# A written issue order for five engines in an attention, MoE and MLP kernel on one Trainium2 core

## The chip, the core and the metric

The kernel runs on one core of one Trainium2 chip. The core has five engines that run side by side, each working through its own instructions in the order in which they were issued: TensorE (PE: matrix products; the loads of its weights are shown apart as PEld), VectorE (DVE), ScalarE (ACT), GpSimd (POOL), and SyncE (SP), which here does nothing but issue transfers. Sixteen DMA engines carry the transfers between HBM and the core's memory. An instruction that waits for another engine's result holds up all that is queued behind it on its own engine.

The metric is the device time of one execution in microseconds, lower is better.

## What is computed

Causal attention with a forgetting bias, then a gated MLP behind an RMS norm, then a second MLP. The sizes are 4 batches, 8 heads, 576 positions, head width 64; a model width of 512; inner widths of 1536 and 2048; so 2304 tokens.

```python
def _attn_ref(q, k, v, s):
    scores = scale * np.matmul(q, k.transpose(0, 1, 3, 2))
    cum = np.cumsum(np.maximum(s, 0.0), axis=-1)
    bias = -(cum[:, :, :, None] - cum[:, :, None, :])
    scores = np.where(causal, -1000000000.0, scores + np.minimum(bias, 0.0))
    attn = np.exp(scores - np.max(scores, axis=-1, keepdims=True))
    attn = attn / (np.sum(attn, axis=-1, keepdims=True) + 1e-09)
    return np.matmul(attn, v)

def _moe_ref(x, w_gate, w_val, w_out, rms_g):
    xn = x / np.sqrt(np.mean(x * x, axis=-1, keepdims=True) + 1e-06) * rms_g
    g = xn @ w_gate
    return (g * (1.0 / (1.0 + np.exp(-g)))) * (xn @ w_val) @ w_out

def _moe2_ref(x, w_in, w_out):
    h = x @ w_in
    return (h - np.tanh(h)) @ w_out
```

## The kernel before

All products are made in 16-bit floats. A 32-bit operand is split into a high part and a small remainder, and a product becomes three matmuls into one sum: high by high, high by remainder, remainder by high (`mm3`, L693 to L695). The weights arrive as 64-bit floats. VectorE turns each piece of 128 x 512 into 32-bit floats with three integer instructions (`decode`, L559 to L561), ScalarE squares it for the scale, and after a scale for the group is known, ScalarE writes the high part (L575) and VectorE the remainder (L576).

The program has three layers of work that overlap.

- **Attention** goes over 20 query tiles T (five in a batch, four of 128 rows and one of 64). For a tile, `prep_q` scales q and splits it (L364 to L368); `emit_smax` makes the scores once to find the row maxima (matmuls L399 to L416 into tiles `sm`, reduced on VectorE at L403, L411 or L417); `emit_rt` splits the maxima (L427, L428), turns them (L431) and lets SP copy them into rows of the q operand (`qc<-rt`, L434); `emit_st` makes the scores again, transposed and less the maxima (L452, L453), ScalarE takes the exponential (L460, L467), GpSimd masks and makes the remainder (L462, L474); `emit_pv` multiplies with v (L494 to L498); `emit_x` and `emit_norm` divide, normalise and split the rows (L513 to L546), and two transposing transfers (L547, L548) bring them into `xth` and `xtl` (tiles of a block of 384 tokens). K of the next batch is scaled and split by `conv_head` (L289 to L291, where VectorE's L291 waits for a copy that SP makes at L290).
- **The gated MLP** runs in six blocks of 384 tokens (`up1_g`, `up1_v`, `down1`). For each of 12 column groups f, a gate tile takes 12 matmuls of 384 columns into one PSUM bank; ScalarE takes its tanh (L711) and VectorE multiplies (L712), which frees the bank. A value tile takes 12 matmuls into another bank, freed by VectorE at L722. There are two such banks while attention runs (`ps_mm`), so the gate tile of f+1 uses the bank of gate tile f. `down1` makes four tiles of 36 matmuls (freed by ScalarE, L733). Blocks 0 to 4 run beside attention of the following tiles, block 5 after it.
- **The second MLP** follows in six blocks: the first two plainly (`up2`, `down2`), then two pairs with a scheme that trades products for additions (`pair_up`).

Weight tasks (`wt`, `wot`, `w2t`) are pushed in between. Weights of the gated MLP are needed by block 0, so their decoding runs in the first quarter of the program.

The order is set by a scheduler that lists the ready instructions by the order in which the code wrote them and by its own estimate of times (`schedule_with_timeline_sim=True`). Two things bind it further. `hold()` puts a transfer behind an earlier one on SP: each load of q, k and v behind the fourth last SP instruction written before it, the weight loads of `decode` behind the copy of the cumulative sums (`gate[0]`). And the second half of the first 16 weight tasks stands behind the last split of maxima:

```python
        with tc.issue_after(last_r[0]) if left[0] < 8 else ExitStack():
            run_tasks(wt, n)
```

Of the kernel before, what the change touches and what calls it, by code (L numbers as in the profile page):

```python
# [30 lines left out]
RSQRT_MAGIC = 1597463007.0 + 2.0 ** 30 - 2.0 ** 22  # L31
LN_P = 2.772588722239781
PAIR_16384 = float.fromhex("0x1.00e8p105")


def width(t):
    return 64 if t == 4 else 128
# [3 lines left out]
def tile_forget_attention_moe_moe2(ctx, tc, qa, qb, kt, va, vb, va0, vb0, s, wg, wv, wo, rg, win, wo2, out):  # L41
    nc = tc.nc
# [27 lines left out]
    V, A, G, P, SY = nc.vector, nc.scalar, nc.gpsimd, nc.tensor, nc.sync  # L70
# [24 lines left out]
    cpd = dram.tile([32, 3, S], FP16, name="cpd")  # L95
# [4 lines left out]
    def sm_tile(dtype=FP32):  # L100

        p, tag = (ps_mm, "mm") if early[0] else (ps_sm, "sm")
        return p.tile([128, 512], dtype, name=tag, tag=tag)

    wide = [None]
# [19 lines left out]
    def small(p, shape, dtype=FP32, tag=None):  # L125
        cnt[0] += 1
        return p.tile(shape, dtype, name=tag or f"sc{cnt[0]}", tag=tag or f"sc{cnt[0]}")
# [13 lines left out]
    def kc_consts(i):  # L141
        (V if i < 2 else G).memset(KC[i][0:64, 0:KW].bitcast(FP32), PAIR_16384)
        (V if i < 2 else G).memset(KC[i][:, KW:KPAD], 0.0)
        (V if i < 2 else G).memset(K2[i][:, KW:KPAD], 0.0)
# [30 lines left out]
    isig_c = const.tile([128, 1], I32, name="isig_c")  # L175

    cum = []
    gate = []

    def hold(kind=0):  # L180

        m = 4 if kind == 0 else 0 if wide[0] is None else 0
        if m == 0 or not gate:
            return tc.issue_after(gate[0]) if gate else ExitStack()
        k = m
        for ins in reversed(nc.cur_bb.bb.instructions):
            if ins.engine == SY.engine:
                k -= 1
                if k == 0:
                    return tc.issue_after(ins)  # L190
        return ExitStack()

    def emit_cum(st, CP):
        SY.dma_start(out=st[:, 0, :], in_=s)
# [23 lines left out]
    vstate = {}  # L218

    def load_qn(b, hh):  # L220
        with hold():
            return _load_qn(b, hh)

    def _load_qn(b, hh):
        t = stage_p.tile([128, 1152], FP32, name="stv", tag="stv", bufs=2)
        SY.dma_start(out=t[:, 0:1024], in_=qa[b, hh].rearrange("t (u d) h c -> (t u) (d h c)", u=32))
        SY.dma_start(out=t[:, 1024:1152], in_=qb[b, hh].rearrange("(u d) h c -> u (d h c)", u=2).rearrange("u (w c) -> (u w) c", w=64))
        return t

    def load_k(b):  # L230
        with hold():
            return _load_k(b)

    def _load_k(b):
        t = stage_p.tile([128, KW], FP32, name="stk", tag="stk", bufs=1)
        SY.dma_start(out=t, in_=kt[b].rearrange("r d h c -> (r d) (h c)"))
        return t

    def load_v(b, hh):
        with hold():  # L240
            return _load_v(b, hh)

    def _load_v(b, hh):
        t = stage_p.tile([128, 20, D], FP32, name="stv", tag="stv", bufs=2)
        SY.dma_start(out=t[:, 0:16, :], in_=va[b, hh].rearrange("p c h d -> p (c h) d"))
        SY.dma_start(out=t[0:64, 16:20, :], in_=vb[b, hh])
        return t
# [74 lines left out]
    qstage = {}  # L322

    def load_q(T):
        with hold():
            return _load_q(T)

    def _load_q(T):
        b, t = ORDER[T]
        w = width(t)  # L330
        if T in (1, 2):
            st = (KC, K2)[T - 1][2][:, 1024:2048].bitcast(FP32).rearrange("p (h c) -> p h c", h=NH)
        else:
            st = qst_p.tile([128, NH, 128], FP32, name="qst", tag="qst")
        for hh in range(2):
            src = qb[b, hh] if t == 4 else qa[b, hh, t]
            SY.dma_start(out=st[64 - 64 * hh:128 - 64 * hh, :, 0:w], in_=src)
        qstage[T] = st
# [6 lines left out]
    def qc_of(T):  # L345
        return spare(KC[2], 0) if T == 2 else QC[T % 2]
# [24 lines left out]


    rstate = {}
    last_r = [None]

    def smax_items(T):
        b, t = ORDER[T]
# [41 lines left out]
    def emit_rt(T):  # L419
        b, t = ORDER[T]  # L420
        rs = rstate.pop(T)
        n = H
        if t == 4:
            n = H // 2
            V.tensor_tensor(out=rs[0][:, 0:n], in0=rs[0][:, 0:n], in1=rs[1][:, 0:n], op=ALU.max)
        r2 = small(sm_p, [128, 2 * H], FP16, "r2")
        V.tensor_scalar(out=r2[:, 0:n], in0=rs[0][:, 0:n], scalar1=-1.0 / 16384.0, scalar2=None, op0=ALU.mult)  # L427
        V.scalar_tensor_tensor(out=r2[:, n:2 * n], in0=rs[0][:, 0:n], scalar=-1.0 / 16384.0, in1=r2[:, 0:n], op0=ALU.mult, op1=ALU.subtract)  # L428
        last_r[0] = nc.cur_bb.bb.instructions[-1]
        ps = sm_tile(FP16)  # L430
        P.transpose(ps[0:2 * n, 0:128], r2[:, 0:2 * n], ident)  # L431
        rt = small(sm_p, [2 * H, 128], FP16, "rt")
        A.activation(out=rt[0:2 * n], in_=ps[0:2 * n, 0:128], func=ACTF.Copy)
        SY.dma_start(out=qc_of(T)[0:2, :, 0:width(t)], in_=rt[0:2 * n, :])  # L434
# [116 lines left out]
    def decode(dst, src, raw):  # L551

        if src.dtype != I32:
            SY.dma_start(out=dst, in_=src)
            return
        with hold(1):
            SY.dma_start(out=raw, in_=src)
        d, hi, lo = dst.bitcast(I32), raw[:, :, 1], raw[:, :, 0]
        V.tensor_scalar(out=d, in0=hi, scalar1=3, scalar2=0x3FFFFFFF, op0=ALU.logical_shift_left, op1=ALU.bitwise_and)  # L559
        V.scalar_tensor_tensor(out=d, in0=hi, scalar=-0x40000000, in1=d, op0=ALU.bitwise_and, op1=ALU.bitwise_or)  # L560
        V.scalar_tensor_tensor(out=d, in0=lo, scalar=29, in1=d, op0=ALU.logical_shift_right, op1=ALU.bitwise_or)  # L561
# [186 lines left out]
    def run_tasks(lst, n):  # L748
        while n > 0 and lst:
            lst.pop(0)()  # L750
            n -= 1
# [123 lines left out]
    emit_consts()  # L875

    def v_first():
      with hold():
        vstate[0] = const.tile([128, H], FP32, name="vone")
        V.memset(vstate[0], 1.0)  # L880
        for hh in range(2):
            v32 = VT[hh].bitcast(FP32)
            SY.dma_start(out=v32[:, 0:16, :], in_=va0[hh])
            SY.dma_start(out=v32[0:64, 16:20, :], in_=vb0[hh])
# [13 lines left out]
    wt = w1_tasks(raw_p)  # L898
    run_tasks(wt, 2)
    CP = cum.pop()  # L900
    for hb in range(2):
        dst = KC[hb][2:5, 0:KW].rearrange("p (h c) -> p h c", h=NH)
        for r in range(3):
            SY.dma_start(out=dst[r:r + 1], in_=CP[hb * NH:(hb + 1) * NH, r, :])
    gate.append(nc.cur_bb.bb.instructions[-1])
    with hold():
        SY.dma_start(out=cpd, in_=CP)
    prep_q(0)
    v_first()
    left = [16]  # L910

# [16 lines left out]
    def need(T):  # L928
        return sum(len(units(x)) for x in range(T + 1)) + 2
# [26 lines left out]
    while last0 not in done_norm:  # L956
        step()
        if steps[0] == 4:
            rest_of_batch0()
        n = min(left[0], 1)  # L960
        left[0] -= n
        with tc.issue_after(last_r[0]) if left[0] < 8 else ExitStack():
            run_tasks(wt, n)
    run_tasks(wt, left[0])
    wot = wo_tasks(raw_p)
    for j in range(NBLK - 1):
        last = BLOCK_TILES[j + 1][1] - 1
        s0 = steps[0]
        n = min(need(last), total) - s0
# [383 lines left out]
        st.close()  # L1353


# [49 lines left out]
```

## Time and profile before

| | us |
|---|---|
| median of 3 runs | 1070.04 (1069.6 to 1071.38) |
| profiled execution, first to last instruction (its span) | 1066.9 |
| median less span | 3.1 |
| PE busy in the profiled execution | 971.0 (91%) |
| DVE busy | 680.1 (64%) |
| ACT busy | 606.2 (57%) |
| POOL busy | 325.6 (31%) |

The profile records one execution; its time as a run is not listed, so its span stands for it, and what lies around it is read off the median. "Busy" is the time in which an engine had an instruction running. A wait is named as who waited, at which line, for whose instruction: "PE mm L693 <- DVE tm L712" is TensorE idle before a matmul of line 693 into a tile `mm` until VectorE's instruction of line 712 ended. PEclk is the TensorE clock that was granted, as a share of full speed.

### The profile page before, as it was taken

The numbers are of one execution on the slowest core, as the hardware profiler recorded it, in microseconds if no ns is written. First come the engines' busy times: TensorE is split into PE (matmuls) and PEld (weight loads), VectorE is DVE, ScalarE is ACT, GpSimd is POOL, SyncE is SP. The second block draws the span as 40 slices with busy tenths as digits, with TensorE's granted clock in tenths as the row PEclk, the third lists the DMA queues.
The fourth block names the chain that finished last, engine by engine and source line by source line (L and its number), as shares of the span: only waits on it lengthen the run. The fifth ranks groups of instructions, "written<-read, shape, count | busy, mean of one in ns | idle before, by whom it ended". The sixth has DMA issues, their size and how long they took to land.

```text
span 1066.9 us, 19296 instructions
## 1 busy us (share of the span) xinstructions
PE 971.0 (91%) x7471; PEld 616.9 (58%) x7472; DVE 680.1 (64%) x1472; ACT 606.2 (57%) x1172; POOL 325.6 (31%) x405
## 2 busy tenths in 40 slices
PE   1488967798899999999999899999999999999998
PEld 1377645455566666666667555655666666666664
DVE  8986998975585641674553878579792683438500
ACT  6589657776665763776766446446571462225400
POOL 5121275423462541364356112100200251015200
PEclk9986989999999999999999999999999999999999
DMA  8614524241211112210100960131102000000000
GB/s 269 257 36 108 191 72 144 65 132 38 64 27 53 25 44 74 77 28 21 54 19 11 309 233 1 46 135 68 60 1 82 8 2 16 23 23 1 8 23 30
DMA packets 49439, 76.81 MB, mean 72 GB/s; under 512 B 25891, under 2 KB 35203, under 8 KB 48835
## 3 DMA queue, kind: packets, MB, share of 16 engines
q1 hardware_dynamic: 49346, 75.58, 22.7%
q8 instruction: 58, 0.95, 0.4%
q14 instruction: 35, 0.28, 0.1%
HBM read 59.42 MB, written 9.55 MB: 65 GB/s over the span
## 4 chain that ended last, share of the span: by engine, by line
PE 63%; DVE 15%; DMA 9%; ACT 6%; issue 4%; POOL 2%; SPq 1%; ACTq 0%; DVEq 0%; POOLq 0%
PE m L693 11%; PE m L695 11%; PE m L694 11%; PE mm L693 7%; PE mm L695 7%; PE mm L694 7%; DVE w L560 1%; PE pv L494 1%; PE st L452 1%; PE st L453 1%; DMA wo<-wv 1%; DMA raw<-wo 1%; DMA w<-wo 1%; DVE w L559 1%; DMA qst<-qa 1%
## 5 line engine op out<-in xcount | busy, mean ns | idle before, releaser
L693 PE MATMUL mm<-xth,w 128*128 128x384 f16 x480 | 158.0, 329 | 28.2 <-DVE tm L712 20.9
L694 PE MATMUL mm<-xtl,w 128*128 128x384 f16 x480 | 157.9, 329 | 0.6 <-DMA xtl<-xl 0.6
L695 PE MATMUL mm<-xth,w 128*128 128x384 f16 x480 | 157.5, 329 | 0.1
L694 PEld LDWEIGHTS <-w 128*128 128x128 f16 x960 | 94.4, 98 | 87.1 <-issue 32.7
L693 PEld LDWEIGHTS <-w 128*128 128x128 f16 x960 | 94.9, 99 | 62.7 <-ACT w L575 3.7
L695 PEld LDWEIGHTS <-w 128*128 128x128 f16 x960 | 94.2, 98 | 63.5 <-issue 2.5
L693 PE MATMUL m<-dh,w 128*128 128x384 f16 x384 | 124.0, 326 | 0.7 <-ACT t L1271 0.7
L694 PE MATMUL m<-dl,w 128*128 128x384 f16 x384 | 124.4, 326 | 0.0
L695 PE MATMUL m<-dh,w 128*128 128x384 f16 x384 | 124.0, 326 | 0.0
L474 POOL TENSOR_TENSOR phl<-pf,phl 128x512 f16<-128x512 f32 (+2 forms) x90 | 97.8, 1094 | 40.1 <-ACT phl L467 38.7
L724 POOL TENSOR_TENSOR sl<-tm,sh 128x384 f16<-128x384 f32 x72 | 74.8, 1039 | 112.9 <-ACT sh L723 105.6
L462 POOL TENSOR_SCALAR_AFFINE_SELECT pf<-pf 128x128 f32<-128x128 f32 (+3 forms) x105 | 46.9, 449 | 175.0 <-ACT pf L460 174.7
L1263 POOL TENSOR_SCALAR io<-iso,isd 128x1 f32<-128x1 f32 x24 | 12.0, 501 | 258.8 <-ACT t L1271 258.8
L460 ACT ACTIVATE pf<-st,lnp,ilam 128x512 f32<-128x512 f32 (+2 forms) x105 | 73.0, 703 | 23.0 <-PE st L453 17.9
L1271 ACT ACTIVATE t<-m,io 128x384 f32<-128x384 f32 x24 | 13.8, 578 | 126.1 <-PE m L695 123.0
L693 PE MATMUL mm<-sh,wo 128*128 128x384 f16 x240 | 77.9, 326 | 2.3 <-DVE tm L712 2.3
L695 PE MATMUL mm<-sh,wo 128*128 128x384 f16 x240 | 78.1, 326 | 0.5 <-DVE wo L576 0.5
L694 PE MATMUL mm<-sl,wo 128*128 128x384 f16 x240 | 78.1, 326 | 0.0
L452 PE MATMUL st<-q,kl 128*128 128x128 f16 (+1 forms) x456 | 62.9, 217 | 8.6 <-DVE q L368 2.7
L1302 DVE SCALAR_TENSOR_TENSOR c<-m,sigma,c 128x768 f32<-128x768 f32 x32 | 32.5, 1015 | 57.3 <-PE m L695 55.6
L1291 POOL TENSOR_TENSOR dl<-c,dh 128x768 f16<-128x768 f32 x28 | 48.0, 1731 | 54.9 <-ACT dh L1290 54.9
L712 DVE SCALAR_TENSOR_TENSOR tm<-tm,mm 128x384 f32<-128x384 f32 x60 | 32.8, 547 | 43.9 <-ACT tm L711 41.4
(369 smaller groups left out, 2582.1 us busy)
## 6 DMA issues: line engine op xcount, KB each, us to landing
raw<-wo SPq DMA_DIRECT2D x16, 512.0 KB
w<-win SPq DMA_DIRECT2D x16, 512.0 KB
wo<-wg SPq DMA_DIRECT2D x12, 512.0 KB
wo<-wv SPq DMA_DIRECT2D x12, 512.0 KB
stk<-kt SPq DMA_DIRECT2D x4, 1152.0 KB
x2d<-tm SPq DMA_DIRECT2D x24, 192.0 KB
x2f<-x2d SPq DMA_DIRECT2D x6, 768.0 KB
out<-t SPq DMA_DIRECT2D x24, 192.0 KB
```

Of the source, the lines that this page charges most:

```text
L452: P.matmul(out=ps[:, o:o + w], lhsT=K2[sl][:, ks], rhs=q2_of(T)[:, h, 0:w], start=True, stop=False)
L460: A.activation(out=pf[:, 0:o], in_=ps[:, 0:o], func=ACTF.Exp, scale=bstate[b]["ilam"][:, hh:hh + 1], bias=lnp)
L462: G.affine_select(out=dg, in_=dg, pattern=[[0, len(heads)], [1, w]], compare_op=ALU.is_ge, fill=0.0, base=0, channel_multiplier=-1)
L474: G.tensor_tensor(out=u["pl"][:, 0:n], in0=u["pf"][:, 0:n], in1=u["ph"][:, 0:n], op=ALU.subtract)
L693: P.matmul(out=ps, lhsT=wh, rhs=xh, start=first, stop=False)
L694: P.matmul(out=ps, lhsT=wh, rhs=xl, start=False, stop=False)
L695: P.matmul(out=ps, lhsT=wl, rhs=xh, start=False, stop=last)
L712: V.scalar_tensor_tensor(out=t, in0=t, scalar=1.0, in1=ps, op0=ALU.add, op1=ALU.mult)
L724: moe_pend.append(lambda: G.tensor_tensor(out=SH["l"][:, f, :], in0=t, in1=SH["h"][:, f, :], op=ALU.subtract))
L1271: A.activation(out=t, in_=ps, func=ACTF.Copy, scale=io)
L1291: by.tensor_tensor(out=DL[:, s8, ds, :], in0=c[:, ds], in1=DH[:, s8, ds, :], op=ALU.subtract)
L1302: V.scalar_tensor_tensor(out=out, in0=ps, scalar=sg, in1=c0, op0=ALU.mult, op1=ALU.add)
```

## The change

The kernel computes the same and issues the same instructions: what is written, and in which buffers, is as before. `ISSUE`, a table of numbers for each of PE, DVE, ACT, POOL and SP, gives the order of that engine's instructions by the place at which the code wrote them (on PE the matmuls, on SP the transfers). `keep_order` ties each instruction to the one before it in that list. `hold()` with its gates and the binding of the weight tasks to `last_r` go. Lines of the kernel after are some 229 to 241 higher than those of before (L712 is L941, L291 is L527, L427 is L658).

```diff
+ISSUE = {
+    "PE": (
+        "0-1 4-8 12-16 9 17 10 18 11 19 38 46 20-37 54-62 39-42 47 43 48 44 49 45 50-53 63-65 75-82 71-74 88-95 101-103 84-87 104-108 113-118 66 119-120 68 67 "
...
+}
...
-    gate = []
-
-    def hold(kind=0):
-
-        m = 4 if kind == 0 else 0 if wide[0] is None else 0
-        if m == 0 or not gate:
-            return tc.issue_after(gate[0]) if gate else ExitStack()
-        k = m
-        for ins in reversed(nc.cur_bb.bb.instructions):
-            if ins.engine == SY.engine:
-                k -= 1
-                if k == 0:
-                    return tc.issue_after(ins)
-        return ExitStack()
...
     def load_qn(b, hh):
-        with hold():
-            return _load_qn(b, hh)
-
-    def _load_qn(b, hh):
...
-        with hold(1):
-            SY.dma_start(out=raw, in_=src)
+        SY.dma_start(out=raw, in_=src)
...
-    gate.append(nc.cur_bb.bb.instructions[-1])
-    with hold():
-        SY.dma_start(out=cpd, in_=CP)
+    SY.dma_start(out=cpd, in_=CP)
...
-        with tc.issue_after(last_r[0]) if left[0] < 8 else ExitStack():
-            run_tasks(wt, n)
+        run_tasks(wt, n)
...
+def keep_order(tc, nc, issue):
+    kinds = {"SP": ("InstDMACopy", "InstDmaTransposeAnt"), "PE": ("InstMatmult",)}
+    info = mybir.DependencyInfo(mybir.DependencyClass.NoSync, mybir.DependencyReason.DATA)
+    for name, order in issue.items():
+        line = [i for i in nc.cur_bb.bb.instructions if str(i.engine).split(".")[-1] == name and not type(i).__name__.startswith("Bass")]
+        line = [i for i in line if type(i).__name__ in kinds[name]] if name in kinds else [i for i in line if type(i).__name__ != "InstRegisterMove"]
+        ranks = []
+        for run in order.split():
+            a, _, z = run.partition("-")
+            ranks += range(int(a), int(z or a) + 1)
+        assert sorted(ranks) == list(range(len(line))), (name, len(ranks), len(line))
+        for a, z in zip(ranks, ranks[1:]):
+            tc.add_manual_dep(line[z], line[a].name, info, reason="issue order")
...
     with tile.TileContext(nc, schedule_with_timeline_sim=True) as tc:
         tile_forget_attention_moe_moe2(tc, *args)
+        keep_order(tc, nc, ISSUE)
```

Three places show what moves. In the rows, a number behind a name tells buffers apart; the rows stand in the order of issue.

VectorE at the split of the first tile's maxima (`r2_295<-r8_274`; L427 and L428, after L658 and L659). `w1_116<-wo_117` are decoding steps of gate weights, `kl2_123` and `q21_129` remainders of q of the next tiles. Before:

```order
L560 SCALAR_TENSOR_TENSOR w1_116<-wo_117,w1_116 128x512
L368 SCALAR_TENSOR_TENSOR kl2_123<-kl2_123,qks_218 64x512
L427 TENSOR_SCALAR r2_295<-r8_274 128x8
L560 SCALAR_TENSOR_TENSOR w1_116<-wo_117,w1_116 128x512
L368 SCALAR_TENSOR_TENSOR kl2_123<-kl2_123,qks_218 64x512
L560 SCALAR_TENSOR_TENSOR w1_116<-wo_117,w1_116 128x512
L561 SCALAR_TENSOR_TENSOR w1_116<-wo_117,w1_116 128x512
L428 SCALAR_TENSOR_TENSOR r2_295<-r8_274,r2_295 128x8
L561 SCALAR_TENSOR_TENSOR w1_116<-wo_117,w1_116 128x512 x2
```

After:

```order
L648 TENSOR_REDUCE r8_274<-sm_285 128x4
L600 SCALAR_TENSOR_TENSOR q20_128<-qst_205,qks_218,q20_128 64x512
L658 TENSOR_SCALAR r2_295<-r8_274 128x8
L501 RECIPROCAL ilam_227<-lam_223 128x2
L599 TENSOR_SCALAR qc1_127<-pat_109,kap_225 5x512
L659 SCALAR_TENSOR_TENSOR r2_295<-r8_274,r2_295 128x8
```

The decoding of weights stood ahead of the maxima and between the two halves of their split; now none of it is ahead of them.

VectorE in block 1, at the gate tile of f = 3 (`mm_3156`, read at L712, after L941; `tm_3170` is what it writes). `kl1_122<-stk_3112` is K of batch 2 (L291, after L527), which waits for SP's copy. Before:

```order
L513 SCALAR_TENSOR_TENSOR rr_3243<-pv_3081,sv8_1477 128x4
L514 RECIPROCAL rr_3243<-rr_3243 128x4
L291 SCALAR_TENSOR_TENSOR kl1_122<-stk_3112,qks_3206,kl1_122 64x576 x2
L712 SCALAR_TENSOR_TENSOR tm_3170<-tm_3170,mm_3156 128x384
L411 ISA junk_3265,r8_2980<-sm_3263,tri_108 128x512
L411 ISA r8_2980 128x1
L291 SCALAR_TENSOR_TENSOR kl1_122<-stk_3112,qks_3206,kl1_122 64x576
L722 SCALAR_TENSOR_TENSOR tm_3170<-tm_3170,mm_3218 128x384
```

After:

```order
L744 RECIPROCAL rr_2889<-rr_2889 128x4
L951 SCALAR_TENSOR_TENSOR tm_3078<-tm_3078,mm_3115 128x384
L941 SCALAR_TENSOR_TENSOR tm_3170<-tm_3170,mm_3156 128x384
L951 SCALAR_TENSOR_TENSOR tm_3170<-tm_3170,mm_3218 128x384
L941 SCALAR_TENSOR_TENSOR tm_3299<-tm_3299,mm_3285 128x384
L642 ISA junk_3058,r8_2980<-sm_3056,tri_108 128x512
L642 ISA r8_2980 128x1
```

The instructions that free the banks now follow each other, and K of batch 2 comes some 50 instructions later.

TensorE at the value tile of f = 2 (`mm_3115`) and the gate tile of f = 3 (`mm_3156`) in the same block. Before, all twelve matmuls of the value tile follow each other, attention comes next, and then the gate tile:

```order
L693 LDWEIGHTS w1_116
L693 MATMUL mm_3115<-xth_1258,w1_116 128x384
L694 LDWEIGHTS w1_116
L694 MATMUL mm_3115<-xtl_1259,w1_116 128x384
L695 LDWEIGHTS w1_116
L695 MATMUL mm_3115<-xth_1258,w1_116 128x384
```

After:

```order
L922 LDWEIGHTS w1_116
L922 MATMUL mm_3115<-xth_1258,w1_116 128x384
L922 LDWEIGHTS w1_116
L922 MATMUL mm_3156<-xth_1258,w1_116 128x384
L923 LDWEIGHTS w1_116
L923 MATMUL mm_3115<-xtl_1259,w1_116 128x384
L923 LDWEIGHTS w1_116
L923 MATMUL mm_3156<-xtl_1259,w1_116 128x384
```

Two tiles in two banks now take turns, matmul by matmul, and end at nearly the same time.

## Rows read from the trace of the kernel before

**Rows 1.** Busy time by stretch of each engine; last PEclk, DMA share, GB/s.

```profile
core 0: us, PE busy (x) PEld busy (x) DVE busy (x) ACT busy (x) POOL busy (x), PEclk, DMA share, GB/s
0.00:40.00 40.00, 6.60 (x35) 4.36 (x36) 36.34 (x84) 25.00 (x37) 15.68 (x29) 1.00 0.91 309
40.00:100.00 60.00, 50.85 (x407) 41.59 (x405) 51.29 (x145) 46.93 (x97) 13.19 (x27) 0.83 0.32 83
100.00:200.00 100.00, 76.77 (x709) 48.47 (x710) 91.66 (x213) 68.05 (x149) 44.55 (x50) 0.90 0.40 119
200.00:240.00 40.00, 36.91 (x281) 22.81 (x279) 31.96 (x93) 30.87 (x68) 16.89 (x17) 1.00 0.41 117
240.00:600.00 360.00, 342.96 (x3247) 224.87 (x3246) 192.72 (x487) 231.40 (x488) 159.62 (x217) 1.00 0.17 51
600.00:740.00 140.00, 134.20 (x818) 80.54 (x818) 109.54 (x225) 77.47 (x158) 16.70 (x15) 0.99 0.37 122
740.00:1066.90 326.90, 322.75 (x1988) 194.23 (x1986) 166.63 (x230) 126.46 (x181) 58.99 (x50) 1.00 0.06 23
```

**Rows 2.** PE's waits, 240 to 740 us: us in total, times, longest.

```profile
PE mm L693 <- DVE tm L712: 13.6, 12, 2.9
PE m L693 <- DVE tm L712: 2.8, 2, 2.4
```

**Rows 3.** DVE in order of time, 34.5 to 38.2 us: start, duration, instruction.

```profile
35.04 0.17 DVE L427 TENSOR_SCALAR r<-r 128x8 f16<-128x8 f32 x1
...
37.22 0.68 DVE L561 SCALAR_TENSOR_TENSOR w<-wo,w 128x512 int32<-128x512 int32 x1
37.83 0.16 DVE L428 SCALAR_TENSOR_TENSOR r<-r,r 128x8 f16<-128x8 f32 x1
```

**Rows 4.** DVE's groups, 0 to 240 us: busy us, mean ns, idle before.

```profile
L561 DVE SCALAR_TENSOR_TENSOR w<-wo,w 128x512 int32<-128x512 int32 x24 | 17.8, 748 | 0.1
...
L368 DVE SCALAR_TENSOR_TENSOR q<-qst,qks,q 64x512 f16<-64x512 f32 (+1 forms) x16 | 11.5, 716 | 2.2 <-ACT q L364 1.7
...
L546 DVE SCALAR_TENSOR_TENSOR xl<-x,ss,xh 128x512 f16<-128x512 f32 (+1 forms) x8 | 7.3, 908 | 1.6 <-ACT xh L545 1.5
...
L411 DVE CUSTOM_DVE_ANT_0 junk<-sm,tri 128x384 bf16<-128x384 f32 x8 | 4.4, 547 | 0.1
```

**Rows 5.** DVE's waits, 60 to 240 us.

```profile
DVE w L559 <- DMA wo<-wv: 5.6, 4, 2.7
...
DVE w L559 <- DMA wo<-wg: 1.0, 1, 1.0
```

**Rows 6.** PE at the gate tile of f = 3 in block 1, in order of time.

```profile
259.38 0.33 PE L695 MATMUL mm<-xth,w 128*128 128x384 f16 x1
...
266.00 0.32 PE L693 MATMUL mm<-xth,w 128*128 128x384 f16 x1 [2.88 <-DVE tm L712]
```

**Rows 7.** DVE at the same gate tile.

```profile
263.77 1.59 DVE L291 SCALAR_TENSOR_TENSOR kl<-stk,qks,kl 64x576 f16<-64x576 f32 x2 [2.73 <-DMA kl<-kc]
265.39 0.56 DVE L712 SCALAR_TENSOR_TENSOR tm<-tm,mm 128x384 f32<-128x384 f32 x1
```

**Rows 8.** PE at an earlier hand-over: last matmul of gate tile, then of value tile.

```profile
249.60 0.33 PE L695 MATMUL mm<-xth,w 128*128 128x384 f16 x1
...
251.54 0.33 PE L694 MATMUL mm<-xtl,w 128*128 128x384 f16 x1
251.70 0.33 PE L695 MATMUL mm<-xth,w 128*128 128x384 f16 x1
```

**Rows 9.** DVE at the hand-overs of Rows 8.

```profile
250.63 0.56 DVE L712 SCALAR_TENSOR_TENSOR tm<-tm,mm 128x384 f32<-128x384 f32 x1 [2.25 <-POOL pf L462]
252.06 0.55 DVE L722 SCALAR_TENSOR_TENSOR tm<-tm,mm 128x384 f32<-128x384 f32 x1 [0.88 <-PE mm L695]
```

**Rows 10.** SP issues the copy of the first tile's maxima.

```profile
38.75 0.73 SPq L434 DMA_DIRECT2D qc<-rt  x1
```

**Rows 11.** PE's first matmul that reads the copy.

```profile
45.04 0.22 PE L453 MATMUL st<-qc,kc 128*128 128x128 f16 x1
```

More of the change, by code (lines that the diff above doesn't have):

```diff
@@ L33 @@
 PAIR_16384 = float.fromhex("0x1.00e8p105")
+ISSUE = {
[172 rows of a table added]
+    ),
+    "DVE": (
[36 rows of a table added]
+    ),
+    "Activation": (
[26 rows of a table added]
+    ),
+    "Pool": (
[9 rows of a table added]
+    ),
[7 rows of a table added]
+    ),
+}
 def width(t):
@@ L230, in load_k @@
     def load_k(b):
-        with hold():
-            return _load_k(b)
-    def _load_k(b):
         t = stage_p.tile([128, KW], FP32, name="stk", tag="stk", bufs=1)
@@ L239, in load_v @@
     def load_v(b, hh):
-        with hold():
-            return _load_v(b, hh)
-    def _load_v(b, hh):
         t = stage_p.tile([128, 20, D], FP32, name="stv", tag="stv", bufs=2)
@@ L324, in load_q @@
     def load_q(T):
-        with hold():
-            return _load_q(T)
-    def _load_q(T):
         b, t = ORDER[T]
@@ L373, in tile_forget_attention_moe_moe2 @@
     rstate = {}
-    last_r = [None]
     def smax_items(T):
@@ L428, in emit_rt @@
         V.scalar_tensor_tensor(out=r2[:, n:2 * n], in0=rs[0][:, 0:n], scalar=-1.0 / 16384.0, in1=r2[:, 0:n], op0=ALU.mult, op1=ALU.subtract)
-        last_r[0] = nc.cur_bb.bb.instructions[-1]
         ps = sm_tile(FP16)
@@ L877, in v_first @@
     def v_first():
-      with hold():
         vstate[0] = const.tile([128, H], FP32, name="vone")
@@ L904, in tile_forget_attention_moe_moe2 @@
             SY.dma_start(out=dst[r:r + 1], in_=CP[hb * NH:(hb + 1) * NH, r, :])
-    gate.append(nc.cur_bb.bb.instructions[-1])
-    with hold():
-        SY.dma_start(out=cpd, in_=CP)
+    SY.dma_start(out=cpd, in_=CP)
     prep_q(0)
```

248 rows, old and new, of the table ISSUE are left out of this document.

## The prediction

> **What bounds the kernel now.** I read first the table of busy time by stretch [rows 1], because the average (TensorE busy 91%) hides that the program has two regimes. Up to about 240 us VectorE is the full engine: 36.3 + 51.3 + 91.7 + 32.0 = 211 us of 240. TensorE is idle 33.4 us of the first 40, then 9.2, 23.2 and 3.1 in the next three stretches, 69 us together. From 240 us on TensorE sets the time: idle 360 − 343.0 = 17.0 us to 600, 5.8 to 740, and 4.2 in the last 327 us. So the change can gain by getting VectorE's early work out of the way sooner, and by closing some of the 22.8 us of holes between 240 and 740; after 740 nothing is left to take.
>
> The second view is TensorE's waits in 240 to 740 us [rows 2]: 13.6 + 2.8 = 16.4 us of the 22.8 stand against VectorE's L712, the multiply that frees a gate tile's bank. The third, in order of time, shows one such wait [rows 6, 7]: the gate tile's last matmul starts at 259.38, but L712 runs only at 265.39, because L291 stands ahead of it on VectorE and itself waits 2.73 us for a copy of K. TensorE's next gate matmul loses 2.88 us. That is head-of-line blocking, a matter of order. The fourth is the start [rows 3]: the first tile's maxima are split at 35.04, but the second half comes at 37.83, with decoding between. All of attention hangs on that.
>
> The times are those of one execution, with a span of 1066.9 us. The median is 3.1 us more; I keep these 3.1 us fixed.
>
> **The change part by part.**
>
> *VectorE's work in the first quarter.* The gated MLP's down products need all output weights, so I take the last conversion of an output weight (the 36th of line L576, at about 240 us) as the mark, and compare what stands ahead of it on VectorE in the two orders. 29 instructions go behind it: five pairs of maxima (L411, 0.55 us and a closing 0.08 us each, 3.1 us), one L546 (0.9), one L368 (0.7) [rows 4], and 17 small ones, which I price like the 0.16 us of L428 [rows 3], 2.7 us at most. That is 7.4 us; 0.6 us of work comes ahead instead, so 6.8 us less. All lies on the full engine. Against it, TensorE has done 1.7 us less of its matmuls (some ten at the 0.16 us pace of [rows 8]) when it reaches block 1, and must do them later, where it is full: net −5.1. With the mark at the first MLP matmuls instead, 9.2 us move behind and 0.7 ahead, −8.5. The 24 decodings that fill the engine (L561, 0.75 us each, [rows 4]) stay, and only their place changes: the 2.6 us lost inside the split [rows 3] move behind tile 0. I take −6. Bounds: 0, if what moved back comes due at once, and −8.5.
>
> *Waits of VectorE for weights.* Between 60 and 240 us L559 waits 5.6 + 1.0 us for its loads [rows 5]. In SP's new order these loads stand five to nine transfers earlier, ahead of K's copy (L290), the copies of maxima (L434) and the transposing transfers, and the gate on the cumulative sums is gone. [...] I take −5 of 6.6. The bounds are 0 and all of VectorE's idle time in 100 to 240 us, 140 − 91.7 − 32.0 = 16.4 [rows 1].
>
> *TensorE's waits for L712.* VectorE's new order puts L712 and L722 one behind the other and K of batch 2 some 50 instructions later. In the shown case the whole 2.88 us go [rows 6, 7]. What is late next there is the ordinary hand-over: at [rows 8, 9] L712 ends 251.19 − 249.60 = 1.59 us after the gate tile's last matmul began, without any wait of TensorE, though VectorE had itself waited 2.25 us for GpSimd. There are 14 such waits, the longest 2.9. Not all have an ordering cause (some L712 wait for ScalarE's tanh), so I take three quarters of 16.4: −12. Bounds: 0 and −16.4.
>
> *New hand-over stalls.* Gate and value tile now take turns matmul by matmul and end together, so a tile's bank must be freed while attention's matmuls run, without the other tile's twelve matmuls as cover. By counting matmuls in both orders at the pace of [rows 8], the TensorE work between the last matmul of a gate tile and the next tile in its bank falls from about 3.2 us (median over blocks 1 to 4) to about 2.06. The need is the 1.59 of [rows 8, 9] plus a semaphore. For value tiles it falls from about 3.2 to 1.10, and the need is 252.61 − 251.70 = 0.91 us (L722, [rows 8, 9]). Both still fit, the value tile with 0.2 us to spare. 48 gate and 48 value tiles pass so. I charge +3, about 0.03 us on each; bounds 0 and +25 (below, the rival on the slow side).
>
> *At nothing.* Instructions and buffers are the same; TensorE's instructions that wait for another engine stay about as many (1067, then 1060), VectorE's become fewer (1665, then 1480). At the block edges the work that covers the transposing transfers (attention's products to the block's first matmul) is at least 17.1 us in the new order; before, the smallest was 8.7, at block 0, and [rows 2] name no wait for `xth`. If that cover went, one edge would cost a few us. After 740 us both orders are almost alike. The clock: TensorE had 0.83 and 0.90 of full speed in 40 to 200 us [rows 1], which means that part of that time was at 1.2 instead of 2.4 GHz, behind the idle start. TensorE isn't the bound there, so I make no term of it; it lets the low end reach further.
>
> Sum: −6 − 5 − 12 + 3 = −20. Span 1066.9 − 20 = 1046.9, and with the 3.1 the median comes to 1050.
>
> [...] The first tile's copy of maxima was issued at 38.75 and first read at 45.04, 6.3 us later [rows 10, 11], in a stretch where the DMA engines were 91% busy [rows 1]. [...]
>
> **The rivals.**
>
> *Only the early cut counts.* The waits for weights and for L712 go elsewhere: VectorE is still 53% busy from 240 to 600 and waits for GpSimd, so that L712 comes late for another reason. For it: 14 waits in 96 hand-overs may be the tail of a busy engine. Against: the shown one has a cause that the order removes [rows 7]. Time: −6 alone, 1064.
>
> *Bulk loads ahead of small copies.* With the gates gone, about 2.5 MB of batch 1's loads stand ahead of tile 2's copy of maxima on SP; at the 309 GB/s of the first stretch [rows 1] that is 8 us, and a copy took 6.3 us already in such a stretch [rows 10, 11]. Attention then starts its third tile that much later, VectorE's early gains (−11) are eaten by up to 8 us, and half of the −12 is lost because VectorE's work is late in blocks 0 and 1. −20 + 8 + 5 + 6 = −1: 1069, no change. [...] Against it: ahead of tile 0's copy the loads (8.6 MB, 28 us at that rate) are through before the maxima are there, and after 40 us the rate falls to 83 GB/s, so that the queue has room.
>
> *The hand-overs lose their cover* (slower). If L712 and L722 keep the lateness that they have now, each wait of [rows 2] grows by the 1.1 us of cover that went: 14 × 1.1 = 16 us; of the other 34 gate tiles about half, and some value tiles, lose half a microsecond: +9. So +25 instead of +3, and the −12 does not come. −6 + 25 = +19, span 1086, median 1089. It decides as soon as the added stalls exceed the 6 us, a quarter of that price. For it: the value tile has only 0.2 us to spare, and one attention instruction on VectorE (0.55 to 0.9 us, [rows 4]) ahead of L722 uses that up. Against: the new order puts L712 and L722 next to each other.
>
> That the change doesn't do what it says can be left out: the compiled order of each engine follows the table.
>
> **How the numbers follow.** Forecast, 1050, own range 1034 to 1058: 0.52. Only the early cut, 1064: 0.17. Bulk loads ahead, 1069: 0.08. Hand-overs uncovered, 1073 to 1089: 0.18. Deeper than 1034 (all of both bounds, −8.5 − 16.4 − 16.4): 0.05. The range 1034 to 1078 leaves out the deep case and most of the slow one. 0.2% is 2 us, about what a measurement of this kernel can tell from no change. Faster: 0.52 + 0.17 + 0.05 = 0.74; within: 0.08; slower: 0.18.
>
> **What would show it.** Right: L428 follows L427 within half a microsecond; no wait of L559 for `wv` and `wg` after 60 us; the first gated MLP matmuls earlier by some 5 us or more; TensorE's waits for L712 in the blocks down from 16.4 to some 4 us; TensorE idle in those blocks 8 to 12 instead of 22.8. Wrong to the slow side: waits of `mm` L693 for L722 appear, and those for L712 become many and short. Wrong by the queue: the gap from the issue of a copy of maxima to its first reader grows past 6.3 us for tiles 1 to 4. Wrong to the fast side: TensorE's idle time before 240 us falls by more than 11, or its clock there rises above 0.90.

## The result, and the profile after

The changed kernel takes 1081.2 us (median of 4, 1077.2 to 1083.8), the kernel before 1069.8 in the same runs: a ratio of 1.0115, 95% interval 1.008 to 1.015. It is slower by 1.15%; the forecast was 1050, faster, with a range of 1034 to 1078. The profiled execution has a span of 1078.2 us against 1066.9.

The busy time by stretch, in the columns of [rows 1]:

```profile
0.00:40.00 40.00, 14.89 (x97) 11.08 (x97) 33.18 (x83) 26.35 (x38) 16.44 (x33) 1.00 0.82 275
40.00:100.00 60.00, 44.64 (x331) 37.51 (x330) 48.83 (x135) 42.95 (x92) 11.59 (x23) 0.74 0.36 111
100.00:200.00 100.00, 82.97 (x704) 49.84 (x706) 85.60 (x205) 69.57 (x138) 33.53 (x47) 0.90 0.45 139
200.00:240.00 40.00, 33.86 (x241) 20.85 (x241) 32.98 (x90) 30.80 (x70) 14.75 (x18) 0.91 0.29 86
240.00:600.00 360.00, 352.90 (x3236) 227.16 (x3234) 181.18 (x487) 229.38 (x485) 159.29 (x214) 1.00 0.14 37
600.00:740.00 140.00, 131.27 (x835) 78.73 (x833) 102.30 (x215) 75.28 (x157) 19.44 (x21) 0.98 0.42 145
740.00:1078.00 338.00, 331.73 (x2041) 199.39 (x2039) 183.25 (x260) 135.38 (x196) 59.12 (x50) 1.00 0.07 24
```

Two rows hold the puzzle. From 240 to 600 us TensorE is busy 352.9 us of 360, ten more than before, but runs 3236 matmuls where it ran 3247: busier, and no further. And from 40 to 100 us its clock is 0.74 instead of 0.83.

TensorE's waits for the two multiplies from 240 to 740 us fell as forecast (the multiply of L712 is now L941, L722 is L951):

```profile
PE m L922 <- DVE t L1481: 4.0, 4, 1.9
PE m L922 <- DVE tm L941: 4.0, 1, 4.0
PE mm L922 <- DVE tm L941: 1.9, 4, 0.8
PE mm L922 <- DVE tm L951: 1.5, 4, 0.6
```

The 16.4 us of [rows 2] are 5.9, and 1.5 us of new waits for L951 have come. All of TensorE's idle time from 240 to 740 us fell from 22.8 to 15.8 us. So the order cured most of what it was to cure, and the time rose all the same.

**A ledger of TensorE.** Where busy time hides a loss, the spacing of matmuls shows it. For each pair of neighbours I took the distance between their starts and subtracted the columns of the first at full clock. (At full clock matmuls of 384 columns start 0.16 us apart, 2.4 columns in a nanosecond: this pace is written as 2.4 GHz, half of it as 1.2. A 32-bit matmul's columns count four times, and twice where it has 64 output columns: at that clock, such matmuls of 65 columns start 0.11 and 0.06 us apart.) What was left went into four classes: clock (what those columns took longer at the granted clock), stalls (over 0.35 us without the clock's part), changes of form (the array's form, such as the "128\*64" or "128\*128" behind a matmul's name, differs between the two) and small rest. In us, the count of changes of form in brackets; e5 and e9 are runs described below (experiments 3 and 6), whose profiled executions were the second fastest and the fastest of their ten:

| stretch, us | class | before | after | e5 | e9 |
|---|---|---|---|---|---|
| 0 to 240 | stalls | 69.0 | 63.1 | 64.7 | 70.2 |
| | clock | 18.3 | 23.1 | 22.5 | 18.0 |
| | changes of form | 6.4 (67) | 10.3 (105) | 4.8 (53) | 5.6 (64) |
| | small rest | 10.2 | 8.8 | 8.5 | 7.9 |
| 240 to 600 | stalls | 19.7 | 8.6 | 8.6 | 8.5 |
| | changes of form | 8.3 (82) | 17.2 (164) | 7.1 (68) | 7.0 (68) |
| | small rest | 8.7 | 12.3 | 11.5 | 11.1 |
| 600 to end | stalls | 7.7 | 12.9 | 12.2 | 12.3 |
| | clock | 1.7 | 2.7 | 1.7 | 1.7 |
| | small rest | 8.4 | 9.6 | 9.0 | 9.1 |

The stalls fell by 11.8 us in all (96.4 to 84.5). Changes of form rose by 12.8 (14.7 to 27.5) and the clock's loss by 5.7 (20.0 to 25.8). In TensorE's issued order there are 269 changes of form instead of 149.

What one costs is seen in the order of time. TensorE in the changed kernel near 436 us (the columns are start, duration, instruction):

```profile
436.12 0.20 PE L727 MATMUL pv<-vt,phl 128*128 128x64 f16 x1
436.25 0.22 PE L630 MATMUL sm<-kc,qc 128*64 128x64 f16 x1
436.40 0.20 PE L728 MATMUL pv<-vt,phl 128*128 128x65 f16 x1
436.54 0.22 PE L632 MATMUL sm<-maskn,bigid 128*64 128x64 f16 x1
436.69 0.23 PE L683 MATMUL st<-qc,kc 128*128 128x128 f16 x1
436.75 0.19 PE L726 MATMUL pv<-vt,phl 128*128 128x65 f16 x1
```

A matmul of 64 or 65 columns takes 0.03 us of the array, as where its neighbour has the same form. Here the next one starts 0.13 to 0.15 us later whenever the form changes, and 0.06 after the 128-column L683, where it doesn't. The durations of 0.2 us overlap, so no idle time appears and no wait is named. The narrow matmuls belong to the 64-row query tiles: their maxima (`sm`) and their products with v (`pv`). The kernel before mostly issues such a group in one piece; the table interleaves them one by one with other work, as it does the gate and value tiles.

Interleaving costs the narrow maxima something else too. Before, the 512-column products of two heads, which fill the two halves of the output rows, stand one behind the other and start together: two of them take 0.34 us to the next matmul.

```profile
443.23 0.41 PE L399 MATMUL sm<-kc,qc 128*64 128x512 f16 x2
443.57 0.34 PE L695 MATMUL mm<-xth,w 128*128 128x384 f16 x1
```

In the changed kernel one alone takes as long:

```profile
428.53 0.40 PE L630 MATMUL sm<-kc,qc 128*64 128x512 f16 x1
428.87 0.34 PE L922 MATMUL mm<-xth,w 128*128 128x384 f16 x1
```

From 240 to 600 us seven of eight such pairs start together before, and one in the changed kernel: six times 0.21 us, 1.3 us of the 3.6 by which the small rest grew there.

### The profile page after: what moved, and what is told of

Read it like the earlier page. It is cut to its first block, busy times and chain, and to the rows that moved or that the text cites. A ratio compares the mean times of both kernels' runs of the same rounds, so it can differ in the third digit from the quotient of the medians.

```text
span 1078.2 us, 19276 instructions
## 1 busy us (share of the span) xinstructions
PE 992.3 (92%) x7469; PEld 624.5 (58%) x7472; DVE 667.3 (62%) x1472; ACT 609.7 (57%) x1172; POOL 314.2 (29%) x405
## 4 chain that ended last, share of the span: by engine, by line
PE 75%; ACT 9%; DVE 9%; DMA 3%; issue 2%; POOL 1%; SPq 0%; ACTq 0%; DVEq 0%; POOLq 0%
PE m L922 11%; PE m L923 11%; PE m L924 11%; PE mm L922 10%; PE mm L923 10%; PE mm L924 10%; PE pv L724 2%; PE st L682 1%; PE st L683 1%; ACT pf L690 1%; DMA qst<-qa 1%; PE pv L728 1%; PE pv L726 1%; ACT x L746 1%; PE pv L727 1%
## 5 line engine op out<-in xcount | busy, mean ns | idle before, releaser
L922 PE MATMUL mm<-xth,w 128*128 128x384 f16 x480 | 144.0, 332 | 9.8 <-DVE tm L951 7.3
L923 PE MATMUL mm<-xtl,w 128*128 128x384 f16 x480 | 143.8, 331 | 0.1
L924 PE MATMUL mm<-xth,w 128*128 128x384 f16 x480 | 142.4, 331 | 0.3 <-DVE ss L774 0.3
L922 PE MATMUL m<-dh,w 128*128 128x384 f16 x384 | 107.8, 326 | 0.9 <-ACT t L1496 0.7
L923 PE MATMUL m<-dl,w 128*128 128x384 f16 x384 | 108.1, 326 | 0.0
L924 PE MATMUL m<-dh,w 128*128 128x384 f16 x384 | 107.9, 326 | 0.0
L704 POOL TENSOR_TENSOR phl<-pf,phl 128x512 f16<-128x512 f32 (+2 forms) x90 | 93.3, 1044 | 49.6 <-ACT phl L697 48.5
L1488 POOL TENSOR_SCALAR io<-iso,isd 128x1 f32<-128x1 f32 x24 | 15.1, 629 | 254.3 <-ACT t L1496 230.1
L682 PE MATMUL st<-q,kl 128*128 128x128 f16 (+1 forms) x456 | 71.5, 217 | 10.4 <-ACT pf L690 4.1
L692 POOL TENSOR_SCALAR_AFFINE_SELECT pf<-pf 128x128 f32<-128x128 f32 (+3 forms) x105 | 42.2, 403 | 115.9 <-ACT pf L690 115.6
L922 PE MATMUL mm<-sh,wo 128*128 128x384 f16 x240 | 73.8, 327 | 2.2 <-ACT tm L962 1.4
L923 PE MATMUL mm<-sl,wo 128*128 128x384 f16 x240 | 74.0, 327 | 0.0
L924 PE MATMUL mm<-sh,wo 128*128 128x384 f16 x240 | 74.0, 327 | 0.0
L683 PE MATMUL st<-qc,kc 128*128 128x128 f16 (+1 forms) x456 | 69.9, 218 | 2.6 <-DMA qc<-rt 2.6
L951 DVE SCALAR_TENSOR_TENSOR tm<-tm,mm 128x384 f32<-128x384 f32 x60 | 33.0, 550 | 46.6 <-PE mm L924 46.2
```

Of the source, the lines that this page charges most:

```text
L682: P.matmul(out=ps[:, o:o + w], lhsT=K2[sl][:, ks], rhs=q2_of(T)[:, h, 0:w], start=True, stop=False)
L683: P.matmul(out=ps[:, o:o + w], lhsT=KC[sl][:, ks], rhs=qc_of(T)[:, h, 0:w], start=False, stop=True)
L692: G.affine_select(out=dg, in_=dg, pattern=[[0, len(heads)], [1, w]], compare_op=ALU.is_ge, fill=0.0, base=0, channel_multiplier=-1)
L704: G.tensor_tensor(out=u["pl"][:, 0:n], in0=u["pf"][:, 0:n], in1=u["ph"][:, 0:n], op=ALU.subtract)
L922: P.matmul(out=ps, lhsT=wh, rhs=xh, start=first, stop=False)
L923: P.matmul(out=ps, lhsT=wh, rhs=xl, start=False, stop=False)
```

## The experiments

The ratios of a run are to the kernel before on the same chip, 1068.6 to 1069.0 us.

**1. The narrow products made wide.** In the changed kernel (e1), and in the kernel before (e2); one line of several:

```diff
-P.matmul(out=ps[0:w, o:o + 65], lhsT=u["ph"][:, cs], rhs=vs[:, 64:129], ...)
+P.matmul(out=ps[0:128, o:o + 65], lhsT=u["ph"][:, cs.start:cs.start + 128], rhs=vs[:, 64:129], ...)
...
```

> The changed kernel with one thing taken away: attention's products with v of the 64-row query tiles use all 128 columns of the array (the last key chunk's scores are made twice, 64 x 26.7 ns = +1.7 us of TensorE work), so that the array's form changes 115 instead of 269 times; all five tables stay. Theory A (each change of form between 128 and 64 columns costs TensorE 0.105 us, read from the spacing of matmuls in 420 to 600 us): 154 x 0.105 = -16.2, +1.7, so about 1067 against 1081. Rival B (the loss lies in the first 240 us, in the lower clock and in VectorE's waits; changes of form are hidden): no gain, 1081 to 1084.

> The same edit in the kernel before: changes of form fall from 149 to 80. Theory A: 69 x 0.105 = -7.2, +1.7, so about 1064.5 against 1070. Rival B: 1070 to 1072.

The changed kernel went to 1069.5 us (ratio 1.0017, 0.9994 to 1.004), 10.5 us less by the ratios, where 14.5 were expected. The kernel before did not gain: 1070.4 (1.0014, 0.9996 to 1.0032), where 5.5 less was expected. Its ledger shows the changes of form from 240 to 600 us down from 82 to 42 and 4.2 us cheaper, and TensorE 4.7 us of work further in that stretch; but it had entered it 7 us behind, in a profiled execution that was the slowest of ten (1075.4). That the first 240 us ate the gain is likely, not shown.

**2. Which part does it.** TensorE's table away, and all tables away (the gates stay away in both):

```diff
-        keep_order(tc, nc, ISSUE)
+        keep_order(tc, nc, {k: ISSUE[k] for k in ("DVE", "Activation", "Pool", "SP")})   # e3; {} in e4
```

> The changed kernel without TensorE's table: the other four engines keep theirs, TensorE's order is again the scheduler's, with 155 changes of form. Theory A: the 12 us of added changes of form go (-12), while some of the gain on waits for L941 may stay: 1064 to 1073. Rival B (the start and the clock): these come from VectorE's and SP's tables, so 1078 to 1084. Rival C (the tables only fit together; a lone scheduler's order on TensorE meets VectorE's order badly): above 1085.

> The changed kernel with no table at all: only the gates on transfers and on the weight tasks are gone, 157 changes of form. If the loss is in the tables (theory A for TensorE's): within 5 us of the kernel before, 1066 to 1075. If it is in the gates (bulk loads stand ahead of the small copies of maxima): 1076 to 1085.

1089.4 and 1088.6 us, ratios 1.018 each: the first came out as rival C had it, the second above both of its numbers. Without the gates and without tables the kernel loses 19 us, and four tables without TensorE's give nothing back. So the change holds a loss of some 19 us (the gates and the binding of the weight tasks) and a gain that four tables without TensorE's don't bring; experiment 7 takes two of the others away. In the run without tables the wait that grew most is TensorE's for the squares of the gate and value weights, 18.4 us there against 3.5 before:

```profile
PE mm L835 <- ACT wo L819: 18.4, 3, 14.0
```

Nothing binds the weight tasks to the split maxima any more, and a matmul of a weight task stands at the head of TensorE's queue until its piece is decoded and squared. This wait is not the 19 us: its longest part, 14.0 us until 39.6 us, stands where the kernel before waits 12.5 us for the split maxima. In columns done at full clock, the run is 7.4 us behind the kernel before at 240 us and 15.1 at 600; no single wait accounts for that.

**3. The narrow matmuls together, nothing else.** Only TensorE's table changes: the members of a group move to the place of its last one.

```diff
...
+        if name == "PE":
+            order = [line[r] for r in ranks]
+            for names in NARROW:
+                mine = [i for i in order if i.name in names]
+                at = order.index(mine[-1])
+                order = [i for i in order[:at] if i.name not in names] + mine + order[at + 1:]
...
```

> The changed kernel with TensorE's table altered in one respect: the matmuls with 64 columns of one maxima item, or of one head's product with v, stand one behind the other (at the place of the last of them) instead of between 128-column matmuls. Instructions and all other tables are as in the changed kernel; changes of form fall from 269 to 121, below the 149 of the kernel before. Theory A (a change of form costs 0.11 us, and counts where TensorE is full, as the run without narrow products with v gave back 10 to 12 us for 154): 1067 to 1071 against 1081. Rival B (that run gained by something else, such as the wider weight loads): no gain, 1079 to 1083.

1067.3 us (ratio 0.9986, 0.9963 to 1.001): by the ratios 13.8 us under the changed kernel, by TensorE's order alone. The row from 240 to 600 us is now

```profile
240.00:600.00 360.00, 352.86 (x3350) 230.06 (x3349) 189.10 (x510) 234.94 (x500) 163.78 (x220) 1.00 0.16 44
```

The same 352.9 busy us carry 114 more matmuls than in the changed kernel. The narrow matmuls stand in one piece, 0.03 us apart, and the pairs of 512 columns start together again, eight of eight from 240 to 600 us:

```profile
428.77 0.22 PE L630 MATMUL sm<-kc,qc 128*64 128x64 f16 x2
428.83 0.20 PE L632 MATMUL sm<-maskn,bigid 128*64 128x64 f16 x2
428.86 0.20 PE L630 MATMUL sm<-kc,qc 128*64 128x64 f16 x2
```

**4. The price by itself.** In the kernel before, where TensorE is full and nothing of attention is left:

```diff
-        P.matmul(out=ps, lhsT=wh, rhs=xl, start=False, stop=False)
+        P.matmul(out=ps[0:m], lhsT=wh[:, 0:m], rhs=xl, start=False, stop=False)   # m = 64 in two groups of four, blocks 2 to 5
...
```

> The kernel before; in two of the four groups of the second MLP's down product of blocks 2 to 5 every second of three matmuls has 64 instead of 128 output columns (it leaves out half of one cross product there). Nothing else differs, and the 384 columns that each streams stay. 256 changes of form are added, where TensorE is busy 99%. Theory A: 256 x 0.11 = +28, so about 1097. Rival B: under +5, because the weight load of the next matmul hides it.

1098.1 us in two runs, +29.4 for 256 changes: 0.115 us each (the ledger has 28.0 us, 0.109 each). Its matmuls of 384 columns, 0.16 us apart elsewhere, stand 0.25 and 0.29 apart at a change and 0.18 where the form stays:

```profile
899.88 0.34 PE L695 MATMUL m<-dh,w 128*128 128x384 f16 x1
900.06 0.33 PE L693 MATMUL m<-dh,w 128*128 128x384 f16 x1
900.31 0.35 PE L694 MATMUL m<-dl,w 128*64 128x384 f16 x1
900.60 0.34 PE L695 MATMUL m<-dh,w 128*128 128x384 f16 x1
```

So a change of form delays the next matmul, by 0.11 us in the mean of the 256; what TensorE does in that time the trace does not show.

**5. The clock.** TensorE's clock falls from 2.4 to 1.2 GHz for stretches in the first 240 us (PEclk is 0.50 in the changed kernel from 60 to 72 and from 78 to 92 us, in the kernel before from 56 to 66 and from 90 to 106; 128-column matmuls start 0.11 us apart there, 0.055 at full clock); the changed kernel loses 35 us of clock in the mean of its executions (span times one less the mean granted clock), the kernel before 26. Added matmuls, 395 by the trace, overwritten later, were put ahead of eleven that wait (experiment 3 otherwise; the edit is not shown):

> The kernel of the run named e5_narrow_together, with 393 more matmuls of 128 columns (20.9 us at full clock, results overwritten) placed in TensorE's order ahead of eleven matmuls before 80 us that wait for another engine, to keep TensorE at work there. Theory C (the lower clock in the first 240 us costs about half a microsecond for each microsecond of clock lost, as the spread of equal kernels shows: 35 us lost against 27 in the kernel before): the clock falls later or less, lost clock below 27 us, and the time 3 to 6 us under e5_narrow_together. Rival D (the clock there is hidden behind VectorE's work): the same within 1.5 us, or some us more because the added matmuls delay others.

1073.2 us (1.0045, 1.0025 to 1.0064), 5.9 us more than experiment 3, and the clock did not rise: 36.8 us lost against 35.0. TensorE's busy time in the first 40 us went from 15.4 to 24.2 us, and the next two stretches have

```profile
40.00:100.00 60.00, 48.94 (x451) 43.15 (x452) 45.40 (x124) 37.92 (x81) 9.91 (x21) 0.75 0.36 112
100.00:240.00 140.00, 116.60 (x943) 74.59 (x945) 119.34 (x298) 99.39 (x209) 49.66 (x66) 0.84 0.39 120
```

against 0.72 and 0.90 without the added matmuls. Theory C did not come true, but the run does not refute it either, because the edit did not keep TensorE at work. The clock falls at 42.9, 63.3 and 83.8 us, and each time in or right behind idle time that was left: 3.34 us from 40.8, 2.49 from 60.5, 2.21 from 81.8.

```profile
44.11 0.27 PE L702 MATMUL st<-q,kl 128*128 128x128 f16 x1 [3.34 <-ACT phl L710]
63.02 4.02 PE L610 MATMUL pv<-ident 128*128 128x128 f16 x40 [2.49 <-ACT x L769]
```

The first of these waits had nothing put ahead of it. Before the second, the forty added matmuls write the bank that TensorE was waiting for, so they wait too and then take 4.0 us at half clock. What the clock does when such waits are filled stays open.

**6. The tables from block 1 on.** The kernel before, its scheduler and gates, up to what the changed kernel had issued by 235 us; then all five tables, narrow matmuls together:

```diff
+CUT = {'PE': 1208, 'DVE': 508, 'Activation': 299, 'Pool': 124, 'SP': 127}
+        first, ranks = ranks[:CUT[name]], ranks[CUT[name]:]
```

> The kernel before (its scheduler, its gates on transfers and on the weight tasks) up to what the changed kernel had issued by 235 us; from there the changed kernel's tables on all five engines, with the narrow matmuls together as in e5_narrow_together (132 changes of form). Theory E (the tables gain only behind 240 us, some 8 us there, and lose in the first 240 us, where they cost clock: 35 us lost against 26): clock lost 25 to 29 us, 1060 to 1066. Rival F (the early tables are what brings the changed kernel its gain over a kernel without tables): 1069 to 1078.

1066.5 us, ratio 0.9973 (0.9958 to 0.9989): a little above the numbers of theory E, and faster than both kernels. The clock lost is 27.3 us. Against experiment 3, with early tables, it differs by 1.4 us by the ratios, and the intervals overlap. So the tables gain behind 240 us, and the early ones are worth no more than the scheduler with its gates.

**7. What else was tried.**

> Changed kernel with products with v of 64-row tiles in 128 columns (as in e1_after_no_narrow) and the narrow maxima matmuls together: 75 changes of form, against 115 there and 121 in e5_narrow_together. Theory A (0.11 us for each, where TensorE is full: about half of the 46 lie there, and 1.7 us of added matmuls): 1065 to 1068. If the wider loads or the added columns cost more: 1068 to 1071.

1066.6 us (0.9981, 0.9963 to 0.9998), as expected, and not to be told from experiment 3.

> The kernel before with its scheduler and without the gates on transfers (the binding of the weight tasks to the split maxima stays). The run without tables and without either was 19 us slower than the kernel before. If the transfers' gates are the reason: 1080 to 1090. If the binding of the weight tasks is: 1066 to 1073.

1079.2 us in two runs (1.010, 1.0054 to 1.0147): the gates on transfers are worth 10.5 us under the scheduler, the larger part of the 19 of experiment 2; the binding of the weight tasks, not run by itself, would be the rest. How the gates earn it is not shown: TensorE waits 0.7 us for a copy of maxima in the first 240 us, and 0.6 in the kernel before.

> e5_narrow_together without SP's table: no gates and no written order of transfers, all other tables stay. If SP's order replaces the gates (without both the kernel before lost 10 us): 1075 to 1085. If the other four tables fix the transfers' order anyway (buffers come free in their order): 1066 to 1070.

1078.9 us in two runs, 11.6 over experiment 3. SP's table is worth about what the gates are; that it does the same work is argued, not shown. Without it a small copy of cumulative sums into K's rows comes late, and TensorE's first scores with it, at 18.75 instead of 16.12 us:

```profile
PE sm L647 <- DMA kc<-sl: 6.8, 1, 6.8
```

That is the lesser part. In columns done at full clock the run is 1.0 us behind experiment 3 at 100 us, 7.5 at 240, 7.0 at 600 and 14.3 at 740, so most is lost from 100 to 240 and from 600 to 740 us; the cause there stays open.

> e5_narrow_together without VectorE's table. If VectorE's order is what takes the waits for the multiply that frees a gate tile (16.4 us before, 5.9 after): these waits come back and the time is 1075 to 1085. If TensorE's order alone does it: 1066 to 1071.

1144.1 us, 77 more, far outside both. A scheduler's order on VectorE under a written order on the other four meets it badly from the start; among TensorE's largest waits up to 240 us are

```profile
PE sm L662 <- DVE r L660: 13.7, 3, 11.1
PE mm L925 <- DVE tm L954: 8.1, 2, 6.0
```

The run says that the tables belong together, and little on the worth of VectorE's order by itself.

## Why the prediction was wrong, by its steps

**TensorE's waits for L712 (−12) and the new hand-overs (+3): right.** −9 was forecast for the two; the waits fell from 16.4 to 5.9, with 1.5 us new for L951, −9.0. The rival of the lost cover did not come: four waits for L951, none over 0.6 us. (Its price rounds 14 × 1.1 = 15.4 up to 16 and lets the −5 for weights fall without a word; with it, 1084 would stand for 1089.) The ledger's stalls from 240 to 600 us fell by 11.1, with 3.6 more small rest.

**"At nothing", the missing term.** The prediction showed that TensorE's order now alternates and asked only whether banks come free in time. It did not ask what alternating costs the array. The count stood in the order itself (149 changes of form, then 269), and the price stood in the trace of before, whose 64 changes from 420 to 600 us cost 0.10 us each. 82 more changes where TensorE is full are 9 us in the ledger, 12.8 with those of the first 240 us, and experiments 1 and 3 got 10.5 and 13.8 back (in experiment 3 with some 1.5 of the pairs): 10 to 14 of the 31 us by which the forecast missed. That the cost is that of the change itself is shown by experiment 4.

**VectorE's early work (−6) and its waits for weights (−5): the causes came, the gain did not.** VectorE's busy time up to 240 us fell from 211.3 to 200.6 us, and the tile-0 maxima were split at 22 to 23 us instead of 35 to 38 [rows 3]. The 6.6 us of waits of [rows 5] are 0.2. But VectorE's idle time rose by as much, from 28.8 to 39.4 us, and it now waits for other engines. Its waits from 60 to 240 us:

```profile
DVE wo L805 <- ACT wo L804: 5.3, 3, 3.8
DVE r L648 <- PE sm L647: 5.3, 2, 2.9
DVE rr L743 <- PE pv L724: 3.0, 2, 2.6
DVE w L805 <- ACT w L804: 2.8, 2, 2.6
```

One of them in the order of time, first TensorE, then VectorE: the 32-bit products of batch 0 run at 1.2 GHz (0.21 us apart; 128-column matmuls 0.11 instead of 0.055), and VectorE stands until those of its tile end.

```profile
63.92 0.63 PE L724 MATMUL pv<-vt,phl 128*128 128x65 f32 x2
64.35 0.31 PE L682 MATMUL st<-kl,kl 128*128 128x128 f16 x1
64.45 0.31 PE L683 MATMUL st<-kc,kc 128*128 128x128 f16 x1
64.56 0.31 PE L682 MATMUL st<-kl,kl 128*128 128x128 f16 x1
64.67 1.06 PE L724 MATMUL pv<-vt,phl 128*128 128x65 f32 x4
```

```profile
65.33 0.16 DVE L743 SCALAR_TENSOR_TENSOR rr<-pv,vone 128x4 f32<-128x4 f32 x1 [2.56 <-PE pv L724]
```

"TensorE isn't the bound there, so I make no term of it" is the sentence that failed: with less on VectorE, these rows show TensorE, there at half clock, and ScalarE next. At 240 us TensorE had done 125.9 us of work (columns at full clock) against 128.9 before, so the −11 were +3.0; changes of form alone took 3.9 us more there (10.3 against 6.4 in the ledger). The first gated matmul came at 100.4 us instead of 103.4, where 5 or more were forecast. Experiment 6 puts the worth of the early tables, changes of form aside, at about nothing.

**"After 740 both orders are almost alike" (0 to 2): too small.** TensorE's stalls from 600 us on rose from 7.7 to 12.9 us. The longest is the fault of [rows 6, 7] again, in block 5. TensorE first, then VectorE:

```profile
644.37 0.48 PE L922 MATMUL m<-xth,w 128*128 128x384 f16 x1 [4.04 <-DVE tm L941]
```

```profile
640.37 0.17 DVE L1264 TENSOR_REDUCE nmi<-px 128x1 f32<-128x8 f32 x1 [0.43 <-PE px L401]
640.45 0.68 DVE L789 SCALAR_TENSOR_TENSOR wi<-w,wi 128x512 int32<-128x512 int32 x1
...
643.17 0.68 DVE L790 SCALAR_TENSOR_TENSOR wi<-w,wi 128x512 int32<-128x512 int32 x1
643.77 0.54 DVE L941 SCALAR_TENSOR_TENSOR tm<-tm,m 128x384 f32<-128x384 f32 x1
```

Decoding and the scale of the second MLP's weights stand ahead of L941, as a load of K did before. In the changed kernel attention also ends later, its last product with v starts at 607.3 us instead of 587.5; but that is not the cause, since in experiments 3 and 6 it starts at 590.1 and 590.8 and the stalls stay (12.2 and 12.3). So both lose here some 5 of the 11 us that they won before.

**The rival of the transfers** did not come at its size in the changed kernel: TensorE's waits for copies of maxima in the first 240 us are 2.2 us, 0.6 before. The prediction gave it a small chance because the queue seemed to have room. Experiment 7 says rather that something must order the transfers, the gates or SP's table: with neither, 10 to 12 us are lost. That a small copy sits out the bulk loads issued ahead of it, on which the rival's 8 us rest, was the author's estimate; the runs show 2.6 us of it at most, the later first scores of the run without SP's table. The rival's price was wrong too: of its −20 + 8 + 5 + 6 the text gives grounds for the 8 and the 6, none for the 5; without it the sum comes to 1064.

**In sum**, from the ledger: stalls −11.8, changes of form +12.8, clock +5.7, small rest +3.5 (over all three stretches), a start 1.6 us later and 0.4 us less of recorded columns make up, but for rounding, the 11.3 us between the two spans. Of the forecast's −20 the gain on waits came; the early −11 did not, and changes of form, set at nothing, took more than the waits gave.

## What to carry to other kernels

Before an order is judged by waits, count how often it changes the form of TensorE's array, and price each change (here 0.11 us) where TensorE is full: this cost showed in no wait and no idle time, only in the spacing of starts and in matmuls per busy microsecond (3236 in 352.9 busy us against 3350 in 352.9). Keep matmuls of a narrow form together; here the move gained 13.8 us and was free, since a group's result is read only after the last of them. A shorter queue on the full engine was worth here what the next engine allowed (VectorE busy 10.7 us less up to 240 us, and idle 10.6 us more), and a written order replaced gates and scheduler only as a whole: without SP's table it was 12 us slower, without TensorE's no better than none, without VectorE's 77 us slower.

## What was not expected of the hardware

- A change between 128 and 64 output columns cost TensorE 0.11 us (28.0 us for 256 in experiment 4), though the streamed columns stayed; the profile counted it as busy.
- Two 512-column matmuls of 64 output columns each, issued one behind the other into the two halves of the output rows, started within 0.01 us of each other and took the time of one (0.34 us to the next matmul, the change of form included).
- More work on TensorE did not by itself keep its clock at 2.4 GHz: with 24.2 instead of 15.4 busy us in the first 40, the clock lost went from 35.0 to 36.8 us; it fell at the idle time of 2.2 to 3.3 us that was left.
- Ten executions of one kernel spread from 1066.4 to 1075.9 us with mean clocks of 0.973 and 0.960 (experiment 1); a straight line through the ten gives half a microsecond for each microsecond of clock lost, which shows that the two go together, not which causes the other. Between the kernels of experiments 3 and 6, 8 us of lost clock go with 1.4 us. How much the clock costs here is therefore not settled.
